# Sliding-window attention on one Trainium2 core: four tokens to an operation in place of two, and logits with a head's eight keys side by side

## The chip, the core and the metric

The kernel runs on one core of a Trainium2 chip. A core has five engines that run their own queues in order: TensorE (PE in the profile; PEld are its weight loads), VectorE (DVE), ScalarE (ACT), GpSimd (POOL) and SyncE (SP), which here issues all DMA transfers. They meet through semaphores. The metric is the device time of the whole program in microseconds. The kernel before took 1144.45 us (median of 3 runs, 1144.21 to 1144.93).

## What is computed

Two layers, each an attention A and an MLP B with residuals, over 2048 tokens of 640 features, in float32. Both layers use the same weights.

```python
def _A_ref(x, wqkv, wo):
    H = 32; Dh = D // H                      # 32 heads of 20
    W, dil = 8, 2
    ...
    idx = pos[:, None] - off[None, :]        # each token sees itself and 7 tokens before it, 2 apart
    ...
    logits = jnp.einsum("bhsd,bhswd->bhsw", q, kg) * scale
    logits = jnp.where(mask[None, None, :, :], logits, -1e9)
    attn = _softmax(logits, axis=-1)
    o = jnp.einsum("bhsw,bhswd->bhsd", attn, vg)
    return (lambda x, *d: x.transpose(*d))(o, 0, 2, 1, 3).reshape(B, S, D) @ wo

def _B_ref(x, w1, b1, w2, b2):
    y = _layernorm(x, axis=-1)
    h = _gelu(jnp.einsum("bsd,df->bsf", y, w1) + b1)
    return jnp.einsum("bsf,fd->bsd", h, w2) + b2

x = x + _A_ref(_layernorm(x, axis=-1), A_wqkv, A_wo)
x = x + _B_ref(_layernorm(x, axis=-1), B_w1, B_b1, B_w2, B_b2)
...
```

## The kernel before

The 2048 tokens of a layer are cut into four units of 512: the even and the odd tokens, in two halves each, since a window steps over every second token. A partition holds four neighbouring tokens of a unit (M = 4). Over the two layers there are eight units, n = 0 to 7. PE works in float16, and each float32 operand is split into a high and a low half: a product is three passes (high by high, high by low, low by high).

For each unit the kernel makes a layer norm, turns it by DMA transposes into `yT`, and multiplies by the query, key and value weights (L648). The result goes to a DRAM buffer (`spill`) and comes back with the seven tokens of halo (`fetch`, L690) in four groups of eight heads, 160 features each (GC = 160); the groups are numbered G = 4n + g, 0 to 31. There is one buffer for queries and keys (`qk`) and one for values (`v`).

Attention of a group runs on DVE. A pass over two tokens (EH = 2), eight keys and 160 features multiplies queries and keys (L732, 2560 elements per partition), and a reduce over the 20 features of a head gives the logits (L736). This is done for both pairs of tokens, in one of two product buffers `pr` each. Then come the mask (L741, in the units that hold the start of the sequence), the maximum over the keys (L744), the subtraction (L745), the exponential on ACT (L747), the sum (L749), its reciprocal (L750) and the product with it (L751). Logits lie token by token, key by key, head by head (`p t w h`), so these two reduces read a head's eight keys at a step of eight elements. The value product (L758) and three halving additions (L766 twice, L770) follow, again for each pair of tokens. ACT and GpSimd (or DVE for the last group, L780) split the result into halves, DMA transposes turn it, and PE multiplies by the output weights (L805, the projection).

The MLP walks over 12 blocks of 128 inner features: an inner product (L871), the GELU on ACT (L877), the high half on ACT (L880), the low half on DVE (L882), and the outer product (L892), whose passes with the high half of the inner block come first and the pass with the low half after. The first unit's MLP is done in two parts of two token tiles each (256 columns), and so has 24 splits L882 of 256 elements; the later ones take 512. The weights are split once at the start, on ACT and DVE (L475, L476), from staging buffers, and parked in DRAM. The last two units are multiplied together by another scheme (`pair`), which reuses the product buffers.

The order on each engine is made when the program is built: `Plan` takes each operation with an estimated duration, a priority and the keys that it needs and gives, and places at every step the operation that can start first, by priority among those ready. A DVE operation is estimated at 0.067 us and 960 elements a microsecond; `more=0.19` is added for the two strided reduces. GpSimd operations marked as a pair wait for a DVE operation with a single input. So a change of sizes moves the work on all engines.

Of the kernel before, what the change touches and what calls it, by code (L numbers as in the profile page):

```python
# [16 lines left out]
P = 128  # L17
# [17 lines left out]
LEAD = (3, 3)  # L35

EH = 2

# [252 lines left out]
def sliding_dilated_then_mlp_kernel(  # L291
# [25 lines left out]
    def many(pool, n, shape, dt, name):  # L317
        return [pool.tile(shape, dt, name=f"{name}{i}") for i in range(n)]
# [69 lines left out]
    for i, q in enumerate(("A12", "S1", "A22", "HL")):  # L388
# [3 lines left out]
        "wq": [("qkvp", last_n, t, g) for t in range(M) for g in range(NG)],  # L392
        "pr": [("o", 2 * NU * NG - 1, a) for a in range(M // EH)] + [("done", 0, i) for i in range(M)],
        "wo": [("wop", last_n, t, c) for t in range(M) for c in range(2)],
# [22 lines left out]
    def dve(n, prio, emit, need=(), give=(), use=(), more=0.0, wait=None):  # L417
        plan.add("dve", v_cost(n) + more, prio, emit, need, give, use, wait=wait, pair=give[0][0] in PAIRS)
# [123 lines left out]
    def layernorm(n, prio, yk, twice):  # L542
# [56 lines left out]
        for t in range(m):  # L599
# [23 lines left out]
            if twice and n != PAIR[0]:  # L623
                G, a = NG * n + ((6, 1), (7, 1), (8, 0), (8, 1))[t][0], (1, 1, 0, 1)[t]
                pool(ASIDE, -200 + n, lambda t=t: nc.gpsimd.tensor_add(x[u][:, t], x[u][:, t], b2),  # L625
                     need=[("y", name, t), ("qk", G, a), "b2"], give=[("xb", n, t)], pair=True)

# [72 lines left out]
    def attention(G):  # L700
        n, g = divmod(G, NG)
        la, u = divmod(n, NU)
        par, start, m = UNITS[u]
        E = EH * W * GC
        L = m * W * GH
        NE = m // EH
# [6 lines left out]
        def windows(w, t0, *dims):  # L713
            c = w[:, t0:t0 + EH]
            return bass.AP(tensor=c.tensor, offset=c.offset, ap=[list(c.ap[0]), [GC, EH], *dims])

        def lg(t0=0, t1=m):
            return tile_of(*sk)[:, t0 * W * GH:t1 * W * GH].rearrange("p (t w h) -> p t w h", t=t1 - t0, w=W)

        def lgt():  # L720
            return lg().rearrange("p t w h -> p t h w")
# [4 lines left out]
        for a in range(NE):  # L726
            t0 = a * EH
            pk = ("pr", (G, a, 0))

            def qk(t0=t0, pk=pk):  # L730
                w = tile_of(*wk)
                nc.vector.tensor_mul(tile_of(*pk), w[:, HALO + m + t0:HALO + m + t0 + EH, None, :].to_broadcast([P, EH, W, GC]),  # L732
                                     windows(w, t0, [GC, W], [1, GC]))

            dve(E, G - 0.6, qk, need=[("inq", G), ("ink", G)], give=[("qk", G, a)], use=[wk, pk, sk])
            dve(E, G - 0.7, lambda pk=pk, t0=t0: nc.vector.tensor_reduce(  # L736
                lg(t0, t0 + EH).rearrange("p t w h -> p (t w h)"), tile_of(*pk).rearrange("p t w (h d) -> p (t w h) d", d=DH),
                axis=AX.X, op=OP.add), need=[("qk", G, a)], give=[("lg", G, a)], use=[pk, sk])
        last = [("lg", G, a) for a in range(NE)]
        if start == 0:  # L740
            dve(L, G - 0.8, lambda: nc.vector.tensor_add(  # L741
                lg(), lg(), mask[:, :, :, None].to_broadcast([P, m, W, GH])), need=[*last, "mask"], give=[("lm", G)], use=[sk])
            last = [("lm", G)]
        dve(L, G - 0.8, lambda: nc.vector.tensor_reduce(mx(0), lgt(), axis=AX.X, op=OP.max), need=last, give=[("mx", G)], use=[sk], more=0.19)  # L744
        dve(L, G - 0.8, lambda: nc.vector.tensor_sub(lg(), lg(), mx(0)[:, :, None, :].to_broadcast([P, m, W, GH])),  # L745
            need=[("mx", G)], give=[("sub", G)], use=[sk])
        act(L, -450 + G, lambda: nc.scalar.activation(tile_of(*sk)[:, :L], tile_of(*sk)[:, :L], AF.Exp, scale=scale),  # L747
            need=[("sub", G)], give=[("e", G)], use=[sk], table="exp")
        dve(L, G - 0.8, lambda: nc.vector.tensor_reduce(mx(1), lgt(), axis=AX.X, op=OP.add), need=[("e", G)], give=[("s", G)], use=[sk], more=0.19)  # L749
        dve(8 * m * GH // 2, G - 0.8, lambda: nc.vector.reciprocal(mx(1), mx(1)), need=[("s", G)], give=[("rc", G)], use=[sk])  # L750
        dve(L, G - 0.8, lambda: nc.vector.tensor_mul(lg(), lg(), mx(1)[:, :, None, :].to_broadcast([P, m, W, GH])),  # L751
            need=[("rc", G)], give=[("at", G)], use=[sk])
        for a in range(NE):
            t0 = a * EH
            vk = ("pr", (G, a, 1))

            def pv(t0=t0, vk=vk):
                nc.vector.tensor_mul(  # L758
                    tile_of(*vk).rearrange("p t w (h d) -> p t (w h) d", d=DH),
                    lg(t0, t0 + EH).rearrange("p t w h -> p t (w h)")[:, :, :, None].to_broadcast([P, EH, W * GH, DH]),  # L760
                    windows(tile_of(*vw), t0, [DH, W * GH], [1, DH]))

            dve(E, G - 0.85, pv, need=[("at", G), ("inv", G)], give=[("pv", G, a)], use=[vw, sk, vk])
            last = ("pv", G, a)
            for w in (4, 2):
                dve(EH * w * GC, G - 0.9, lambda vk=vk, w=w: nc.vector.tensor_add(  # L766
                    tile_of(*vk)[:, :, 0:w], tile_of(*vk)[:, :, 0:w], tile_of(*vk)[:, :, w:2 * w]),
                    need=[last], give=[("ad", G, a, w)], use=[vk])
                last = ("ad", G, a, w)
            dve(EH * GC, G - 0.9, lambda vk=vk, t0=t0: nc.vector.tensor_add(  # L770
                ot()[:, t0:t0 + EH], tile_of(*vk)[:, :, 0], tile_of(*vk)[:, :, 1]),
                need=[last], give=[("o", G, a)], use=[vk, ok])

        def hi():
            return tile_of(*hk)[:, :, 0, g * GC:(g + 1) * GC]

        act(m * GC, -350 + G, lambda: nc.scalar.activation(hi(), ot(), AF.Copy),
            need=[("o", G, a) for a in range(NE)], give=[("oh", G)], use=[ok, hk])
        def lo(eng):
            eng.tensor_sub(tile_of(*hk)[:, :, 1, g * GC:(g + 1) * GC], ot(), hi())  # L780

        if g < NG - 1:
            pool(ASIDE, -300 + G, lambda: lo(nc.gpsimd), need=[("oh", G), ("qk", G + 1, 0)], give=[("ol", G)], use=[ok, hk],
                 pair=True)
        else:
            dve(m * GC, -300 + G, lambda: lo(nc.vector), need=[("oh", G)], give=[("ol", G)], use=[ok, hk])
# [561 lines left out]
```

## Time and profile before

| | |
|---|---|
| median of 3 runs | 1144.45 us |
| span of the profiled execution | 1146.1 us |
| granted TensorE clock, mean | 0.998 |
| DVE products L732 and L758 | 64 each, 2808 and 2818 ns |
| DVE reduce L736 | 64, 2801 ns |
| DVE additions L766 | 128, 1150 ns |
| moved by DMA | 235.47 MB, mean 205 GB/s |

The profiled execution is one run under the hardware profiler; its span is that of the program's instructions. A group of instructions has its line, engine, output and inputs by the program's names, the count, and the mean duration. Idle time of an engine matters only where another one waits for it.

### The profile page before, as it was taken

Reading aid. Unit: us, or ns where it says so; the run is one execution under the profiler, and the core shown is the slowest. Engines: PE = TensorE matmul, PEld = TensorE weight load, DVE = VectorE, ACT = ScalarE, POOL = GpSimd, SP = SyncE. Lnnn points to the kernel's source line nnn. Section 1 sums busy time; section 2 is a strip of 40 time slices with the busy share of each in tenths; the row PEclk is TensorE's granted clock in tenths of the full one; section 3 lists DMA queues with packets and bytes.
Section 4 is the critical chain, followed back from the end, with each engine's and each line's share of the span. In section 5 each row is a group of like instructions: output and inputs, shape, how many; then the busy total and the mean of one; then the engine's idle time right before and its main releaser. Section 6 shows DMA issues by size and latency. Waiting matters only on the chain.

```text
span 1146.1 us, 17470 instructions
## 1 busy us (share of the span) xinstructions
PE 1137.1 (99%) x6812; PEld 628.4 (55%) x6812; DVE 1038.4 (91%) x1028; ACT 606.6 (53%) x1131; POOL 113.2 (10%) x94
## 2 busy tenths in 40 slices
PE   9999999999999999999999999999999999999998
PEld 6444446567565465546555555556455556555476
DVE  7999999999899999999999999999999993847972
ACT  6485336536365275734537662479347445657720
POOL 1010000211111102110112012012111000000000
PEclk9999999999999999999999999999999999999999
DMA  9999998978976477576655965569686555974201
GB/s 318 307 299 266 329 302 244 321 264 244 239 189 232 140 221 213 178 207 198 186 187 176 221 190 164 175 188 192 164 247 183 175 171 156 217 239 122 65 24 69
DMA packets 239791, 235.47 MB, mean 205 GB/s; under 512 B 139020, under 2 KB 195164, under 8 KB 239708
## 3 DMA queue, kind: packets, MB, share of 16 engines
q1 hardware_dynamic: 239708, 234.36, 69.9%
q8 instruction: 53, 0.87, 0.3%
q14 instruction: 30, 0.25, 0.1%
HBM read 157.55 MB, written 44.78 MB: 177 GB/s over the span
## 4 chain that ended last, share of the span: by engine, by line
PE 72%; DVE 3%; DMA 1%; issue 0%; ACT 0%; DVEq 0%
PE acc L892 18%; PE ps L871 17%; PE ps L648 17%; PE ps L805 10%; PE acc L1073 4%; PE ps L1108 3%; PE ps L1073 2%; DMA yT<-w 1%; DVE yT L1020 1%; DVE pr L1005 1%; PE acc L1108 1%; DVE wq L1194 0%; DVE wq L1182 0%; DVE v L1195 0%; DVE xf L1196 0%
## 5 line engine op out<-in xcount | busy, mean ns | idle before, releaser
L648 PE MATMUL ps<-wq,yT 128*128 128x480 f16 (+1 forms) x1950 | 391.0, 363 | 1.5 <-DMA yT<-w 1.1
L648 PEld LDWEIGHTS <-yT 128*128 128x128 f16 x1950 | 189.3, 98 | 200.8 <-DMA yT<-w 1.4
L892 PE MATMUL acc<-c,act 128*128 128x512 f16 (+1 forms) x1728 | 249.3, 299 | 2.3 <-DMA c<-mw 1.6
L871 PE MATMUL ps<-yT,c 128*128 128x512 f16 (+1 forms) x1260 | 247.8, 350 | 0.0
L892 PEld LDWEIGHTS <-act 128*128 128x128 f16 x1728 | 136.1, 98 | 108.8 <-issue 1.9
L871 PEld LDWEIGHTS <-c 128*128 128x128 f16 x1260 | 120.9, 98 | 107.3 <-DMA c<-mw 0.3
L732 DVE TENSOR_TENSOR pr<-qk 128x2560 f32<-128x2560 f32 x64 | 179.5, 2808 | 0.0
L758 DVE TENSOR_TENSOR pr<-sm,v 128x2560 f32<-128x2560 f32 x64 | 179.1, 2818 | 0.3
L736 DVE TENSOR_REDUCE sm<-pr 128x128 f32<-128x2560 f32 x64 | 179.2, 2801 | 0.0
L665 ACT ACTIVATE ev<-ps 128x480 f32<-128x480 f32 x128 | 72.6, 568 | 177.2 <-PE ps L648 157.5
L877 ACT ACTIVATE act<-ps,b 128x512 f32<-128x512 f32 (+1 forms) x84 | 52.4, 624 | 172.9 <-PE ps L871 170.2
L766 DVE TENSOR_TENSOR pr<-pr 128x640 f32<-128x640 f32 (+1 forms) x128 | 143.1, 1150 | 0.3
L805 PE MATMUL ps<-wo,yT 128*128 128x320 f16 x960 | 131.7, 299 | 0.0
L805 PEld LDWEIGHTS <-yT 128*128 128x128 f16 x960 | 93.8, 98 | 37.4
L780 POOL TENSOR_TENSOR ohl<-w,ohl 128x640 f16<-128x640 f32 x24 | 34.9, 1456 | 425.9 <-DVE pr L732 171.6
L882 DVE TENSOR_TENSOR act<-act 128x512 f16<-128x512 f32 (+1 forms) x84 | 51.0, 609 | 16.0 <-ACT act L880 15.9
L587 POOL TENSOR_TENSOR ln<-ln,half 128x2 f32<-128x2 f32 (+1 forms) x31 | 36.2, 1173 | 276.6 <-ACT ln L584 276.6
L625 POOL TENSOR_TENSOR xf<-xf,b 128x640 f32<-128x640 f32 x24 | 37.3, 1558 | 144.6 <-DVE pr L732 58.4
L880 ACT ACTIVATE act<-act 128x512 f16<-128x512 f32 (+1 forms) x84 | 47.5, 565 | 3.4 <-PE acc L892 1.5
L610 ACT ACTIVATE w<-xf,ln 128x640 f32<-128x640 f32 x53 | 47.5, 909 | 2.7 <-DVE w L618 2.1
L570 ACT ACTIVATE junk<-xf 128x640 f16<-128x640 f32 x57 | 41.8, 733 | 12.9 <-DVE xf L814 8.0
L618 DVE TENSOR_TENSOR w<-w,w 128x640 f16<-128x640 f32 x56 | 45.7, 830 | 2.1 <-ACT w L616 2.1
(200 smaller groups left out, 984.1 us busy)
## 6 DMA issues: line engine op xcount, KB each, us to landing
c<-mw SPq DMA_DIRECT2D x174, 320.0 KB, 3.6
spill<-ev SPq DMA_DIRECT2D x64, 480.0 KB, 3.6
qk<-spill SPq DMA_DIRECT2D x32, 880.0 KB, 6.0
v<-spill SPq DMA_DIRECT2D x32, 880.0 KB, 5.3
qk<-spill SPq DMA_DIRECT2D x32, 320.0 KB, 3.6
act<-in_B_w_dram SPq DMA_DIRECT2D x24, 320.0 KB, 4.9
mw<-c SPq DMA_DIRECT2D x24, 320.0 KB, 4.7
pr<-in_B_w_dram SPq DMA_DIRECT2D x24, 320.0 KB, 4.1
```

The costliest lines, as they stand in the source:

```text
L648: nc.tensor.matmul(ps, transposed(yk)[:, a * KD + k, t * P:(t + 1) * P], wq[:, b, k, g, i0:i1], start=first and j == 0, stop=last and j == ...
L665: act(3 * GC, -400 + n, lambda i=i, pk=pk, ek=ek: nc.scalar.activation(tile_of(*ek)[:, :, i], tile_of(*pk)[:, :3 * GC].rearrange("p (a c) ...
L732: nc.vector.tensor_mul(tile_of(*pk), w[:, HALO + m + t0:HALO + m + t0 + EH, None, :].to_broadcast([P, EH, W, GC]), windows(w, t0, [GC, W], ...
L736: dve(E, G - 0.7, lambda pk=pk, t0=t0: nc.vector.tensor_reduce(lg(t0, t0 + EH).rearrange("p t w h -> p (t w h)"), tile_of(*pk).rearrange(" ...
L758: nc.vector.tensor_mul(tile_of(*vk).rearrange("p t w (h d) -> p t (w h) d", d=DH), lg(t0, t0 + EH).rearrange("p t w h -> p t (w h)")[:, :, ...
L766: dve(EH * w * GC, G - 0.9, lambda vk=vk, w=w: nc.vector.tensor_add(tile_of(*vk)[:, :, 0:w], tile_of(*vk)[:, :, 0:w], tile_of(*vk)[:, :, w ...
L805: nc.tensor.matmul(tile_of(*pk)[:, :D // 2], transposed(yk)[:, a * KD + k, t * P:(t + 1) * P], wo[:, b, k, c * D // 2:(c + 1) * D // 2], s ...
L871: nc.tensor.matmul(tile_of(*pk)[:, :nt], tile_of(*ck)[:, a, k * P:(k + 1) * P], transposed(yk)[:, c * KD + k, t0 * P:t1 * P], start=i == 0 ...
L877: act(nt, -430, lambda pk=pk, h32=h32, e=e: nc.scalar.activation(tile_of(*h32)[:, :nt], tile_of(*pk)[:, :nt], AF.Gelu_apprx_tanh, bias=b1[ ...
L882: dve(nt, -1000, lambda h32=h32, hk=hk: nc.vector.tensor_sub(tile_of(*hk)[:, 1, :nt], tile_of(*h32)[:, :nt], tile_of(*hk)[:, 0, :nt]), nee ...
L892: nc.tensor.matmul(accs[k][:, c0:c0 + n], tile_of(*hk)[:, a, (i - t0) * P:(i - t0 + 1) * P], tile_of(*wk)[:, c, w0:w0 + n], start=first, s ...
L1073: nc.tensor.matmul(tile_of(*to(i))[:, :HALF], hl()[:, a, i * P:(i + 1) * P], row(c), start=start and (a, c) == PASS[0], stop=(a, c) == PAS ...
```

## The change

Attention no longer works on pairs of tokens. One product buffer holds all four tokens, key by key (`pr`, 8 keys x 4 tokens x 160 features); its two halves by keys still serve as the two staging buffers elsewhere. The query-key product, the reduce, the value product and each of the additions are one operation over 5120, 5120, 5120, 2560, 1280 and 640 elements. The logits are laid out token by token, head by head, key by key (`p t h w`), so that a head's eight keys are neighbours; the first reduce writes them at a step of eight elements and the value product reads them so. The maximum and the sum read neighbouring elements and lose `more=0.19`. Keys in the plan lose their pair number, and with them the needs of GpSimd's operations.

```diff
-        "pr": many(sb, SLOTS["pr"], [P, EH, W, GC], FT, "pr"),
...
+    pr = sb.tile([P, W, M, GC], FT, name="pr")
+    T["pr"] = [pr[:, i * W // 2:(i + 1) * W // 2] for i in range(2)]
...
-                G, a = NG * n + ((6, 1), (7, 1), (8, 0), (8, 1))[t][0], (1, 1, 0, 1)[t]
+                G = NG * n + (6, 7, 8, 8)[t]
...
-        E = EH * W * GC
+        E = m * W * GC
...
+        def lg():
+            return tile_of(*sk)[:, :L].rearrange("p (t h w) -> p t h w", t=m, w=W)
+
+        def by_key():
+            return tile_of(*sk)[:, :L].rearrange("p (x w) -> p w x", w=W)
...
+        def heads():
+            return pr.rearrange("p w t (h d) -> p w (t h) d", d=DH)
...
+            nc.vector.tensor_mul(pr.rearrange("p w t c -> p w (t c)"),
+                                 w[:, HALO + m:HALO + 2 * m].rearrange("p t c -> p (t c)")[:, None, :].to_broadcast([P, W, m * GC]),
+                                 windows(w, [1, m * GC]))
...
+        dve(E, G - 0.7, lambda: nc.vector.tensor_reduce(by_key(), heads(), axis=AX.X, op=OP.add),
...
-        dve(L, G - 0.8, lambda: nc.vector.tensor_reduce(mx(0), lgt(), axis=AX.X, op=OP.max), need=last, give=[("mx", G)], use=[sk], more=0.19)
+        dve(L, G - 0.8, lambda: nc.vector.tensor_reduce(mx(0), lg(), axis=AX.X, op=OP.max), need=last, give=[("mx", G)], use=[sk])
...
+        dve(E, G - 0.85, lambda: nc.vector.tensor_mul(
+            heads(), by_key()[:, :, :, None].to_broadcast([P, W, m * GH, DH]), windows(tile_of(*vw), [DH, m * GH], [1, DH])),
+            need=[("at", G), ("inv", G)], give=[("pv", G)], use=[vw, sk, *vk])
+        last = ("pv", G)
+        for w in (4, 2):
+            dve(m * w * GC, G - 0.9, lambda w=w: nc.vector.tensor_add(pr[:, 0:w], pr[:, 0:w], pr[:, w:2 * w]),
...
+        dve(m * GC, G - 0.9, lambda: nc.vector.tensor_add(ot(), pr[:, 0], pr[:, 1]), need=[last], give=[("o", G)], use=[*vk, ok])
```

The planner's order moves with it. The lines of the changed kernel are numbered anew: L730 is the query-key product, L735 its reduce, L742 and L747 the maximum and the sum, L743 the subtraction, L751 the value product, L756 and L759 the additions, L869 the MLP split that was L882. In the rows, `sm` holds logits and weights, `pr` products, `act` the MLP's inner block.

DVE's queue in the second group of heads, before, from the maximum to the next product (the exponential on ACT stands between L745 and L749; L618 splits a layer norm's result):

```order
L744 TENSOR_REDUCE sm_90<-sm_90 128x32
L745 TENSOR_TENSOR sm_90<-sm_90 128x256
L618 TENSOR_TENSOR w_88<-w_85,w_88 128x640
L749 TENSOR_REDUCE sm_90<-sm_90 128x32
L750 RECIPROCAL sm_90<-sm_90 128x32
L751 TENSOR_TENSOR sm_90<-sm_90 128x256
L732 TENSOR_TENSOR pr_76<-qk_67 128x2560
```

And now, from the maximum L742 to the sum L747:

```order
L742 TENSOR_REDUCE sm_88<-sm_88 128x32
L759 TENSOR_TENSOR w_85<-pr 128x640
L743 TENSOR_TENSOR sm_88<-sm_88 128x256
L730 TENSOR_TENSOR pr<-qk_67 128x5120
L617 TENSOR_TENSOR w_84<-w_83,w_84 128x640
L475 SCALAR_TENSOR_TENSOR wo<-act,wo 128x640
L747 TENSOR_REDUCE sm_88<-sm_88 128x32
```

Between the subtraction and the sum stood one split of 640 elements; now a whole query-key product of the next group, a split L617 and a weight split L475 stand there.

DVE's queue at the first splits of the MLP, before:

```order
L758 TENSOR_TENSOR pr_77<-sm_90,v_68 128x2560
L882 TENSOR_TENSOR act<-act 128x256 x2
L766 TENSOR_TENSOR pr_77<-pr_77 128x2x640
L882 TENSOR_TENSOR act<-act 128x256
L766 TENSOR_TENSOR pr_77<-pr_77 128x2x320
L758 TENSOR_TENSOR pr_76<-sm_90,v_68 128x2560
L770 TENSOR_TENSOR w_85<-pr_77 128x320
L766 TENSOR_TENSOR pr_76<-pr_76 128x2x640
L745 TENSOR_TENSOR sm_89<-sm_89 128x256
L766 TENSOR_TENSOR pr_76<-pr_76 128x2x320
L732 TENSOR_TENSOR pr_77<-qk_67 128x2560
L882 TENSOR_TENSOR act<-act 128x256
```

And now:

```order
L730 TENSOR_TENSOR pr<-qk_67 128x5120
L869 TENSOR_TENSOR act<-act 128x256
L747 TENSOR_REDUCE sm_87<-sm_87 128x32
L735 TENSOR_REDUCE sm_88<-pr 128x8x32
L869 TENSOR_TENSOR act<-act 128x256
L748 RECIPROCAL sm_87<-sm_87 128x32
L742 TENSOR_REDUCE sm_88<-sm_88 128x32
L749 TENSOR_TENSOR sm_87<-sm_87 128x256
L743 TENSOR_TENSOR sm_88<-sm_88 128x256
L869 TENSOR_TENSOR act<-act 128x256
L751 TENSOR_TENSOR pr<-sm_87,v_68 128x5120
```

The first three splits stood within four rows, with one addition between. Now each of the first two has an operation over 5120 elements ahead of it.

DVE's queue from the thirteenth and fourteenth split (the first row with L882) to the seventeenth (the last row); L936 and L923 add the MLP's result to the residual, L767 splits the attention's result of a unit's last group. Before:

```order
L736 TENSOR_REDUCE sm_89<-pr_77 128x128
L882 TENSOR_TENSOR act<-act 128x256 x2
L936 SCALAR_TENSOR_TENSOR xf<-acc_101,xf 128x2x128
L936 SCALAR_TENSOR_TENSOR xf<-acc_97,xf 128x512
L882 TENSOR_TENSOR act<-act 128x256
L936 SCALAR_TENSOR_TENSOR xf<-acc_98,xf 128x512
L751 TENSOR_TENSOR sm_90<-sm_90 128x256
L758 TENSOR_TENSOR pr_76<-sm_90,v_68 128x2560
L882 TENSOR_TENSOR act<-act 128x256
L766 TENSOR_TENSOR pr_76<-pr_76 128x2x640
L766 TENSOR_TENSOR pr_76<-pr_76 128x2x320
L882 TENSOR_TENSOR act<-act 128x256
```

And now, where the last row holds the seventeenth and the eighteenth:

```order
L735 TENSOR_REDUCE sm_87<-pr 128x8x32
L869 TENSOR_TENSOR act<-act 128x256 x2
L923 SCALAR_TENSOR_TENSOR xf<-acc_100,xf 128x2x128
L923 SCALAR_TENSOR_TENSOR xf<-acc_96,xf 128x512
L923 SCALAR_TENSOR_TENSOR xf<-acc_97,xf 128x512
L767 TENSOR_TENSOR ohl_75<-w_83,ohl_75 128x4x160
L739 TENSOR_TENSOR sm_87<-sm_87,mask 128x256
L730 TENSOR_TENSOR pr<-qk_67 128x5120
L869 TENSOR_TENSOR act<-act 128x256 x2
L742 TENSOR_REDUCE sm_87<-sm_87 128x32
L735 TENSOR_REDUCE sm_88<-pr 128x8x32
L869 TENSOR_TENSOR act<-act 128x256 x2
```

A value product with its two additions stood ahead of the seventeenth split; now a query-key product and a reduce of the tenth group stand there, and the split L767 of the second unit.

More of the change, by code (lines that the diff above doesn't have):

```diff
@@ L35 @@
 LEAD = (3, 3)
-EH = 2
 FAST = {0: (0, 1, 2), 1: (0, 1, 2, 3)}
@@ L711, in ot, with windows @@
             return tile_of(*ok).rearrange("p (t c) -> p t c", t=m)
[L713 to L721, printed above, removed]
+        def windows(w, *dims):
+            return bass.AP(tensor=w.tensor, offset=w.offset, ap=[list(w.ap[0]), [GC, W], *dims])
@@ L740, in attention @@
+        dve(E, G - 0.6, qk, need=[("inq", G), ("ink", G)], give=[("qk", G)], use=[wk, *pk, sk])
+        dve(E, G - 0.7, lambda: nc.vector.tensor_reduce(by_key(), heads(), axis=AX.X, op=OP.add),
+            need=[("qk", G)], give=[("lg", G)], use=[*pk, sk])
+        last = [("lg", G)]
         if start == 0:
             dve(L, G - 0.8, lambda: nc.vector.tensor_add(
-                lg(), lg(), mask[:, :, :, None].to_broadcast([P, m, W, GH])), need=[*last, "mask"], give=[("lm", G)], use=[sk])
+                lg(), lg(), mask[:, :, None, :].to_broadcast([P, m, GH, W])), need=[*last, "mask"], give=[("lm", G)], use=[sk])
@@ L748, in attention @@
             need=[("sub", G)], give=[("e", G)], use=[sk], table="exp")
[L749 removed]
+        dve(L, G - 0.8, lambda: nc.vector.tensor_reduce(mx(1), lg(), axis=AX.X, op=OP.add), need=[("e", G)], give=[("s", G)], use=[sk])
         dve(8 * m * GH // 2, G - 0.8, lambda: nc.vector.reciprocal(mx(1), mx(1)), need=[("s", G)], give=[("rc", G)], use=[sk])
[L751 removed]
+        dve(L, G - 0.8, lambda: nc.vector.tensor_mul(lg(), lg(), mx(1)[:, :, :, None].to_broadcast([P, m, GH, W])),
@@ L774, in hi @@
+        last = ("pv", G)
+        for w in (4, 2):
+            dve(m * w * GC, G - 0.9, lambda w=w: nc.vector.tensor_add(pr[:, 0:w], pr[:, 0:w], pr[:, w:2 * w]),
+                need=[last], give=[("ad", G, w)], use=vk)
+            last = ("ad", G, w)
+        dve(m * GC, G - 0.9, lambda: nc.vector.tensor_add(ot(), pr[:, 0], pr[:, 1]), need=[last], give=[("o", G)], use=[*vk, ok])
         def hi():
@@ L777, in attention @@
         act(m * GC, -350 + G, lambda: nc.scalar.activation(hi(), ot(), AF.Copy),
-            need=[("o", G, a) for a in range(NE)], give=[("oh", G)], use=[ok, hk])
+            need=[("o", G)], give=[("oh", G)], use=[ok, hk])
         def lo(eng):
```

42 lines of the change are left out of this document (7 added, 35 removed).

## The prediction

> **What bounds the kernel now.** The page comes first: which engine is full, and who ends the chain.
>
> ```profile
> span 1146.1 us, 17470 instructions
> PE 1137.1 (99%) x6812; PEld 628.4 (55%) x6812; DVE 1038.4 (91%) x1028; ACT 606.6 (53%) x1131; POOL 113.2 (10%) x94
> ...
> PE 72%; DVE 3%; DMA 1%; issue 0%; ACT 0%; DVEq 0%
> ```
>
> TensorE (PE) is busy for all but 9.0 us of the span, and the change leaves its matmuls alone. What can be won is time in which PE stands still; what can be lost is new time of that kind. So the next view is the waits of PE, and with it the windows in which its busy time is short of 50.
>
> ```profile
> PE acc L892 <- DMA c<-mw: 1.6, 2, 1.3
> PE acc L1269 <- POOL ident L447: 1.3, 1, 1.3
> PE ps L648 <- DMA yT<-w: 1.1, 1, 1.1
> PE acc L892 <- DVE act L882: 0.7, 1, 0.7
> ```
>
> ```profile
> 50.00:100.00 50.00, 50.00 (x249) 24.17 (x247) 47.97 (x44) 40.31 (x86) 5.04 (x5) 1.00 0.98 291
> 100.00:150.00 50.00, 50.00 (x249) 24.16 (x247) 46.94 (x41) 16.72 (x29) 2.80 (x2) 1.00 0.96 322
> 150.00:200.00 50.00, 50.00 (x288) 27.99 (x287) 48.04 (x38) 27.82 (x61) 1.72 (x2) 1.00 0.88 263
> 200.00:250.00 50.00, 48.01 (x314) 29.87 (x313) 50.00 (x44) 23.40 (x43) 10.08 (x7) 0.97 0.91 286
> 250.00:300.00 50.00, 48.58 (x371) 33.04 (x370) 45.94 (x51) 24.93 (x50) 6.50 (x4) 1.00 0.93 252
> ```
>
> In each row the second number is PE's busy time, the fourth VectorE's (DVE), and the third from the end the granted clock. PE loses 1.99 us in 200:250, 1.5 us more there to a clock of 0.97 (3% of 50), and 1.42 us in 250:300: **4.9 us** in all, at the start of the first MLP block and just before the second layer's first product. DVE is idle for 7.05 us in 50:200 and not at all in 200:250. So DVE sets the pace here beside PE, and the change is about DVE.
>
> **The price of one DVE operation.** The timeline, start and duration in us:
>
> ```profile
> 229.17 2.82 DVE L758 TENSOR_TENSOR pr<-sm,v 128x2560 f32<-128x2560 f32 x1
> 231.90 0.48 DVE L770 TENSOR_TENSOR w<-pr 128x320 f32<-128x320 f32 x1
> 232.30 1.49 DVE L766 TENSOR_TENSOR pr<-pr 128x1280 f32<-128x1280 f32 x1
> 233.71 0.42 DVE L745 TENSOR_TENSOR sm<-sm 128x256 f32<-128x256 f32 x1
> 234.04 0.82 DVE L766 TENSOR_TENSOR pr<-pr 128x640 f32<-128x640 f32 x1
> 234.78 2.82 DVE L732 TENSOR_TENSOR pr<-qk 128x2560 f32<-128x2560 f32 x1
> ...
> 238.25 0.42 DVE L882 TENSOR_TENSOR act<-act 128x256 f16<-128x256 f32 x1
> 238.59 0.61 DVE L749 TENSOR_REDUCE sm<-sm 128x32 f32<-128x256 f32 x1
> 239.11 2.81 DVE L736 TENSOR_REDUCE sm<-pr 128x128 f32<-128x2560 f32 x1
> ...
> 242.17 0.35 DVE L750 RECIPROCAL sm<-sm 128x32 f32<-128x32 f32 x1
> 242.43 2.77 DVE L732 TENSOR_TENSOR pr<-qk 128x2560 f32<-128x2560 f32 x1
> ```
>
> The next operation starts about 0.08 us before the last one's duration is over, so I price by the step from start to start: 2.73 for 2560 elements, 1.41 for 1280, 0.74 for 640, 0.40 for 320, 0.33 for 256, 0.52 for the strided reduce of 256, 0.26 for the reciprocal. From 1.41 and 0.74 the part that doesn't grow with the elements is 0.07. A 5120-element operation, which the trace doesn't have, is then 2 x 2.73 - 0.07 = 5.39, between 5.34 (no fixed part at all) and 5.46 (twice the half); the low end is the nearer, since 1280 against 640 shows the fixed part is paid once.
>
> Fewer instructions: six pairs of a group become one each, 192 of 1028. A group cost 6 x 2.73 + 2 x (1.41 + 0.74 + 0.40) + 1.96 = 23.44 us (1.96 is the softmax: 0.52, 0.33, 0.52, 0.26, 0.33). It will cost 3 x 5.39 + 2.75 + 1.41 + 0.73 + 1.58 = 22.64, where the two reduces of the softmax now read side by side and are taken at 0.33 like L745. That is 0.80 a group, 25.6 us over 32 groups. [...] None of this is on the path by itself: PE's 1137.1 us covers it.
>
> An operation that needs the one just ahead of it takes longer:
>
> ```profile
> 292.89 0.62 DVE L744 TENSOR_REDUCE sm<-sm 128x32 f32<-128x256 f32 x1
> 293.54 0.42 DVE L745 TENSOR_TENSOR sm<-sm 128x256 f32<-128x256 f32 x1
> ```
>
> The step is 0.65 in place of 0.52, so 0.125 each. Ahead of the first MLP split 29 operations stand so in the old order and 9 in the new: 2.5 us saved.
>
> **What moves.** PE waits for DVE through the splits L882 (the low half of the MLP's inner block). In the new order 5.39 us pieces stand between them, and more attention stands ahead of them. Ahead of the first split the old queue has groups 0 to 4 whole, 15.61 us of group 5 and 11.44 of group 6: 144.2 us. The new one has groups 0 to 5 whole, 11.44 of group 6 and 5.39 of group 7: 152.7. Ahead of the seventeenth: 7 groups, 17.76 of the eighth and 5.46 of the ninth, 187.3, against 8 groups, 11.44 and 10.78, and one L780 at 0.74: 204.1. So the new queue is 8.4 and then 16.8 us longer at the same work of PE, 5.9 and **14.3** after the 2.5.
>
> ```profile
> 225.11 1.80 PE L871 MATMUL ps<-yT,c 128*128 128x256 f16 x15
> 226.02 0.76 DVE L882 TENSOR_TENSOR act<-act 128x256 f16<-128x256 f32 x2
> 226.74 2.55 PE L892 MATMUL acc<-c,act 128*128 128x512 f16 x17
> ...
> 277.29 0.42 DVE L882 TENSOR_TENSOR act<-act 128x256 f16<-128x256 f32 x1
> ...
> 282.48 1.79 PE L892 MATMUL acc<-c,act 128*128 128x512 f16 x12
> ...
> 284.11 0.60 PE L871 MATMUL ps<-yT,c 128*128 128x256 f16 x4
> ```
>
> The seventeenth split ended at 277.71. Eight of the 12 matmuls at 282.48 use the high half (12 take 1.63 us, so 1.09), so PE needed it at 283.57: 5.86 us to spare. 14.3 - 5.86 = 8.4 us late, less what DVE gets back of its idle time. At the first split 0.86 us was to spare (226.44 against 226.74 plus four matmuls, 0.54), and the 15 matmuls at 225.11, 1.63 us, now stand behind it: 5.9 - 0.86 + 1.63 = 6.7 late, less the same.
>
> How much comes back:
>
> ```profile
> DVE c L476 <- ACT c L475: 3.5, 6, 1.1
> DVE sm L749 <- ACT sm L747: 2.3, 4, 0.8
> DVE w L618 <- ACT w L616: 0.3, 1, 0.3
> ```
>
> These are DVE's waits between 50 and 200 us. The exponential's wait (2.3) is covered in the new order by a 5.39 us product from the second group on, so 1.8 of it goes. The weight splits' wait (3.5) goes where they stand behind more attention, as 19 of 29 do by at least part of an operation. Bounds: 1.8 (exponentials alone) and 7.05 (all idle time of the windows). I take **5.5**, nearest to the 6.1 that the three rows add up to, because attention fills most of these gaps.
>
> Sum: 8.4 - 5.5 = 2.9 us later at the seventeenth split than the old PE was, with the old stalls already in that time. The 1.42 us at 290 go, since the wait there (L648 for yT) falls behind a PE that is 2.9 us later. From there DVE only gains on PE. Total +1.5 us on the profiled 1146.1, or 1147.6; that execution is 1.65 above the median of 1144.45, so **1146.0**: no change. What a measurement of this kernel can tell from no change is 0.2%, 2.3 us.
>
> At nothing I cost: GpSimd's adds (10% busy; the reduce that lets them in is now one of 5.39), the tail (attention ends earlier, the last products still run through PE), and the copies ACT makes. If that cover were gone, a GpSimd add of some 1.5 us would be late once a unit, eight times.
>
> **Rivals.** *Faster:* the splits are late nowhere, and all 4.9 us go: 1139.6. It takes DVE regaining more than the 8.4, beyond its 7.05 us of idle, or ACT being late as well; with half of the 4.9, 1142.0. For it speaks that the new PE order puts the first low-half matmuls ahead of a product that could have filled a wait. I give it 0.19.
>
> *Slower, at the MLP start:* the weights arrive no earlier (DMA share 0.96 to 0.98), so only the 1.8 comes back: 8.4 - 1.8 - 1.4 = +5.2, 1149.7. It is slower by over 0.2% from a return under 4.7 on. The third unit's projection is a second place of this kind:
>
> ```profile
> 405.01 0.82 DVE L780 TENSOR_TENSOR ohl<-w,ohl 128x640 f16<-128x640 f32 x1
> ...
> 413.27 6.79 PE ps L805 x50
> ```
>
> 7.4 us lie between DVE's last piece and PE; PE comes 22.3 us of matmuls sooner, DVE's queue is 14.9 shorter (12.4 by these prices and the 2.5), so nothing is left but the returned 5.5 and PE's own lateness, for the transposes that stand between. Chance 0.29.
>
> *The layout costs what it saves:* logits are now written, and weights read, at a step of eight elements, as L749 reads them: 0.52 against 0.33, 0.19 for 256 elements. Taken once for each reduce and each value product, 18 stand ahead of the seventeenth split: 3.4 us, 1149.4. Against it: each such element is followed by 19 more cycles of the same. Chance 0.10. [...] That the softmax reduces stay at 0.52 would be the same 3.0 us by the eighth group, and is counted in this chance.
>
> **How the numbers follow.** The forecast has 0.42. Same is 0.40 of it; faster 0.20, the faster rival and a sliver of the forecast; slower 0.40, the two slower rivals and another sliver. The range goes from a little beyond half of the faster rival, 1141.0, to 1152.5, which is the slower rival with the layout's 3.4 less a little.
>
> **What the new profile would show.** A 5120-element step of 5.39 and a group of 22.6 us, DVE at about 1012 busy (1038.4 - 25.6). PE short by some 5 to 7 us in 200:300 with DVE's L869 as releaser, and full afterwards. If PE stands nowhere in 200:300, the return was underrated; if it stands at projections near 390 to 520, the second place decides; if the value product's step is over 5.5, the layout does.

## The result and the profile after

The changed kernel took 1153.43 us (median of 4 runs, 1151.19 to 1153.65) against 1144.38 for the kernel before: a ratio of 1.0071, 95% interval 1.0059 to 1.0084. It is slower by 0.7%. The forecast was 1146.0 and the range ended at 1152.5. The profiled execution took 1151.19 us, with a span of 1149.4. Each run of the changed kernel has both numbers, and in all of them the time is the span and about 1.8 us.

The page of the changed kernel, the busy times and the products:

```profile
span 1149.4 us, 17270 instructions
...
PE 1136.1 (99%) x6812; PEld 627.4 (55%) x6812; DVE 1024.6 (89%) x836; ACT 603.7 (53%) x1129; POOL 152.0 (13%) x94
...
L730 DVE TENSOR_TENSOR pr<-qk 128x5120 f32<-128x5120 f32 x32 | 175.5, 5484 | 19.9 <-DMA qk<-spill 19.5
...
L751 DVE TENSOR_TENSOR pr<-sm,v 128x5120 f32<-128x5120 f32 x32 | 175.8, 5492 | 0.4
L735 DVE TENSOR_REDUCE sm<-pr 128x256 f32<-128x5120 f32 x32 | 175.3, 5477 | 0.2
...
L767 POOL TENSOR_TENSOR ohl<-w,ohl 128x640 f16<-128x640 f32 x24 | 59.2, 2465 | 400.1 <-DVE pr L730 223.1
...
L617 DVE TENSOR_TENSOR w<-w,w 128x640 f16<-128x640 f32 x56 | 50.9, 924 | 7.0 <-ACT w L615 6.9
```

DVE does less (1024.6 busy after 1038.4) with 192 instructions fewer, and PE's work is the same. The span has 13.3 us without PE, 4.3 more than before. PE's waits and windows in the changed kernel:

```profile
PE acc L879 <- DVE act L869: 6.0, 5, 3.0
...
PE acc L879 <- ACT act L867: 0.9, 1, 0.9
PE ps L858 <- DMA c<-mw: 0.6, 1, 0.6
```

```profile
50.00:100.00 50.00, 50.00 (x249) 24.15 (x248) 49.10 (x34) 39.29 (x84) 6.41 (x5) 1.00 1.02 303
100.00:150.00 50.00, 50.00 (x249) 24.15 (x248) 49.79 (x33) 18.64 (x33) 3.25 (x2) 1.00 1.00 297
150.00:200.00 50.00, 50.00 (x288) 28.05 (x287) 49.46 (x32) 29.42 (x66) 2.00 (x2) 1.00 0.92 276
200.00:250.00 50.00, 45.57 (x302) 27.54 (x300) 49.86 (x37) 24.71 (x43) 8.26 (x7) 1.00 0.99 312
250.00:300.00 50.00, 46.86 (x380) 34.05 (x379) 48.83 (x43) 22.47 (x48) 12.09 (x4) 1.00 0.88 252
```

PE is short by 4.43 and 3.14 us in the last two rows, 7.57 in all, at the start of the first MLP block, and the split L869 releases it in five of the waits. DVE's idle time between 50 and 200 went from 7.05 to 1.65, so 5.4 us came back. The timeline of DVE shows what each late split stands behind:

```profile
222.57 5.49 DVE L730 TENSOR_TENSOR pr<-qk 128x5120 f32<-128x5120 f32 x1
227.98 0.42 DVE L869 TENSOR_TENSOR act<-act 128x256 f16<-128x256 f32 x1
228.31 0.41 DVE L747 TENSOR_REDUCE sm<-sm 128x32 f32<-128x256 f32 x1
228.64 5.48 DVE L735 TENSOR_REDUCE sm<-pr 128x256 f32<-128x5120 f32 x1
234.04 0.41 DVE L869 TENSOR_TENSOR act<-act 128x256 f16<-128x256 f32 x1
...
248.47 5.49 DVE L751 TENSOR_TENSOR pr<-sm,v 128x5120 f32<-128x5120 f32 x1
253.88 1.95 DVE L869 TENSOR_TENSOR act<-act 128x256 f16<-128x256 f32 x2
...
287.94 0.75 DVE L869 TENSOR_TENSOR act<-act 128x256 f16<-128x256 f32 x2
```

The last row holds the seventeenth split. And PE's timeline, with its idle time in brackets:

```profile
225.72 1.26 PE L879 MATMUL acc<-c,act 128*128 128x512 f16 x8 [0.93 <-ACT act L867]
228.46 1.80 PE L879 MATMUL acc<-c,act 128*128 128x512 f16 x12 [1.47 <-DVE act L869]
...
234.51 2.53 PE L879 MATMUL acc<-c,act 128*128 128x512 f16 x16 [0.97 <-DVE act L869]
...
255.56 0.72 PE L879 MATMUL acc<-c,act 128*128 128x512 f16 x4 [2.98 <-DVE act L869]
...
287.49 1.79 PE L879 MATMUL acc<-c,act 128*128 128x512 f16 x12
```

The first wait is for the high half, which ACT makes (L867). Each of the three waits for L869 ends with a split that had a 5.4 us operation ahead of it. The longest has something more: two splits take 1.95 us where two others take 0.75. GpSimd's timeline has the reason:

```profile
248.61 6.61 POOL L767 TENSOR_TENSOR ohl<-w,ohl 128x640 f16<-128x640 f32 x1 [17.45 <-DVE sm L749]
```

Such a subtraction takes 1.40 us at its shortest and 1.64 in the median of the 24. This one came 0.14 us after the value product and ended 1.3 us after it, so it seems to have been held by the product, and the split by it. One profile cannot tell that from a late start; an experiment can.

### The profile page after: what moved, and what is told of

It reads as the page before. It is cut to its first block, busy times and chain, and to the rows that moved or that the text cites. A ratio compares the mean times of both kernels' runs of the same rounds, so it can differ in the third digit from the quotient of the medians.

```text
span 1149.4 us, 17270 instructions
## 1 busy us (share of the span) xinstructions
PE 1136.1 (99%) x6812; PEld 627.4 (55%) x6812; DVE 1024.6 (89%) x836; ACT 603.7 (53%) x1129; POOL 152.0 (13%) x94
## 4 chain that ended last, share of the span: by engine, by line
PE 89%; DVE 7%; issue 2%; ACT 1%; DMA 0%; SPq 0%; DVEq 0%; ACTq 0%
PE ps L647 31%; PE acc L879 19%; PE ps L858 19%; PE ps L792 11%; PE acc L1060 3%; PE ps L1095 3%; PE ps L1060 2%; DVE pr L992 1%; DVE pr L756 1%; DVE pr L751 1%; DVE pr L730 1%; DVE sm L735 1%; DVE yT L1007 1%; PE acc L1095 1%; DMA xf<-in_A_x_dram 0%
## 5 line engine op out<-in xcount | busy, mean ns | idle before, releaser
L730 DVE TENSOR_TENSOR pr<-qk 128x5120 f32<-128x5120 f32 x32 | 175.5, 5484 | 19.9 <-DMA qk<-spill 19.5
L751 DVE TENSOR_TENSOR pr<-sm,v 128x5120 f32<-128x5120 f32 x32 | 175.8, 5492 | 0.4
L735 DVE TENSOR_REDUCE sm<-pr 128x256 f32<-128x5120 f32 x32 | 175.3, 5477 | 0.2
L756 DVE TENSOR_TENSOR pr<-pr 128x2560 f32<-128x2560 f32 x64 | 140.8, 2200 | 0.2
L767 POOL TENSOR_TENSOR ohl<-w,ohl 128x640 f16<-128x640 f32 x24 | 59.2, 2465 | 400.1 <-DVE pr L730 223.1
L586 POOL TENSOR_TENSOR ln<-ln,half 128x2 f32<-128x2 f32 (+1 forms) x31 | 50.0, 1616 | 320.5 <-ACT ln L583 320.5
L869 DVE TENSOR_TENSOR act<-act 128x512 f16<-128x512 f32 (+1 forms) x84 | 53.0, 640 | 13.5 <-ACT act L867 13.1
L617 DVE TENSOR_TENSOR w<-w,w 128x640 f16<-128x640 f32 x56 | 50.9, 924 | 7.0 <-ACT w L615 6.9
L624 POOL TENSOR_TENSOR xf<-xf,b 128x640 f32<-128x640 f32 x24 | 38.2, 1601 | 85.3 <-DVE pr L730 39.3
L867 ACT ACTIVATE act<-act 128x512 f16<-128x512 f32 (+1 forms) x84 | 47.4, 565 | 1.8
```

The source lines that it names most:

```text
L730: nc.vector.tensor_mul(pr.rearrange("p w t c -> p w (t c)"), w[:, HALO + m:HALO + 2 * m].rearrange("p t c -> p (t c)")[:, None, :].to_broa ...
L735: dve(E, G - 0.7, lambda: nc.vector.tensor_reduce(by_key(), heads(), axis=AX.X, op=OP.add), need=[("qk", G)], give=[("lg", G)], use=[*pk, sk])
L751: dve(E, G - 0.85, lambda: nc.vector.tensor_mul(heads(), by_key()[:, :, :, None].to_broadcast([P, W, m * GH, DH]), windows(tile_of(*vw), [ ...
L756: dve(m * w * GC, G - 0.9, lambda w=w: nc.vector.tensor_add(pr[:, 0:w], pr[:, 0:w], pr[:, w:2 * w]), need=[last], give=[("ad", G, w)], use=vk)
L869: dve(nt, -1000, lambda h32=h32, hk=hk: nc.vector.tensor_sub(tile_of(*hk)[:, 1, :nt], tile_of(*h32)[:, :nt], tile_of(*hk)[:, 0, :nt]), nee ...
```

## Experiments

Three theories were open. **Layout:** the new writes and reads cost time. **Long pieces:** operations of 5.4 us hold up the splits, in any order. **Order:** the planner, given other durations, comes out with an order that is worse around the first MLP block. Beside these stood the GpSimd subtraction, and the question how far the two profiled executions stand for their kernels. The kernel before was timed again beside each of three sets of runs, with medians of 1144.87, 1144.73 and 1144.91 us; the last run below stands beside a single one of 1143.74.

### Both kernels again

> The kernel before, unchanged, for a second profile. All four executions of the changed kernel took 1.75 to 1.8 us more than their span. If that holds for the old kernel too, the profiled execution with its span of 1146.1 took about 1147.9, and was 3.4 us above its median, and the 3.41 us in which PE was short in 200:300 and the dip of the clock were of that execution alone. Theory 'typical execution has no stalls': this profile has a span of 1142.4 to 1143.2 and PE is short by under 1.0 us in 200:300. Theory of the prediction, that these stalls are the kernel's own: span 1145.5 to 1146.5, PE short by about 3.4 us there again. Time 1144.4 by both.

> The changed kernel, unchanged, for a second profile: its first one has a span of 1149.4 where three other executions had 1151.6 to 1151.9. [...] Time 1153.4.

The kernel before: 1145.15 us (10 runs, 1144.02 to 1148.53). Its profiled execution was the slowest of the ten, 1148.53. Its span, and its windows:

```profile
span 1146.8 us, 17470 instructions
```

```profile
200.00:250.00 50.00, 48.83 (x337) 30.94 (x335) 50.00 (x44) 24.31 (x45) 10.14 (x7) 1.00 0.94 298
250.00:300.00 50.00, 47.17 (x355) 31.67 (x354) 46.81 (x51) 24.34 (x49) 6.43 (x4) 1.00 0.90 245
```

PE is short by 4.0 us there, and by 1.52 in 400:450. Read alone, this is the profile of the other theory, that the stalls are the kernel's own. But the other nine executions have spans of 1142.2 to 1144.9. This one has 10.8 us of span without PE, 5.5 of them in these stalls; if nothing else differs, a span of 1142.2 has room for only 0.9 us of stalls, and one of 1144.9 for 3.6. So the stalls differ from execution to execution, and both profiles of the old kernel are of executions that have many of them. This is worked out from the spans: no quick execution of this kernel was profiled.

The changed kernel: 1151.95 us (4 runs, 1151.25 to 1154.24), ratio 1.0066 (1.0051 to 1.0081). PE is short by 7.6 us in 200:300, at the same places, and by 0.3 in 500:550. This execution (1151.64) is one of the quick ones too, so where the longer ones lose 2.2 to 2.6 us more than the profiled execution of their set was not seen.

### Layout and order, each alone

The layout alone, with two tokens to an operation:

```diff
-        "pr": many(sb, SLOTS["pr"], [P, EH, W, GC], FT, "pr"),
+        "pr": many(sb, SLOTS["pr"], [P, W, EH, GC], FT, "pr"),
...
-            return tile_of(*sk)[:, t0 * W * GH:t1 * W * GH].rearrange("p (t w h) -> p t w h", t=t1 - t0, w=W)
+            return tile_of(*sk)[:, :L].rearrange("p (t h w) -> p t h w", t=m, w=W)
...
-        dve(L, G - 0.8, lambda: nc.vector.tensor_reduce(mx(0), lgt(), axis=AX.X, op=OP.max), need=last, give=[("mx", G)], use=[sk], more=0.19)
+        dve(L, G - 0.8, lambda: nc.vector.tensor_reduce(mx(0), lg(), axis=AX.X, op=OP.max), need=last, give=[("mx", G)], use=[sk])
```

> The layout alone: products key by key and logits with a head's eight keys side by side, but two tokens to an operation as before. Theory 'pieces' (the loss comes from operations of 5.4 us between the splits and from their order): 1143.5 to 1145, no change or a little faster, DVE busy about 12 us less than before (64 strided reduces at 0.19). Theory 'layout' (the strided writes and reads cost, or the order that the cheaper reduces bring): 1149 to 1153.

1150.04 us, ratio 1.0044 (1.0028 to 1.0059): taken by itself a win for "layout". But PE's waits name another releaser:

```profile
PE ps L874 <- DMA c<-mw: 4.3, 2, 3.0
```

Weights for the first block land late; the row names no DVE operation. The planner had lost its 0.19 for the two reduces (the last pair of lines of the diff), and with it the order had changed. So the layout and the order were taken apart. The kernel before without the 0.19 has in every queue, row by row, the order of the layout run (the sum's line L749 is changed in the same way):

```diff
-        dve(L, G - 0.8, lambda: nc.vector.tensor_reduce(mx(0), lgt(), axis=AX.X, op=OP.max), need=last, give=[("mx", G)], use=[sk], more=0.19)
+        dve(L, G - 0.8, lambda: nc.vector.tensor_reduce(mx(0), lgt(), axis=AX.X, op=OP.max), need=last, give=[("mx", G)], use=[sk])
```

The layout run with the 0.19 kept has the order of the kernel before:

```diff
-        dve(L, G - 0.8, lambda: nc.vector.tensor_reduce(mx(0), lg(), axis=AX.X, op=OP.max), need=last, give=[("mx", G)], use=[sk])
+        dve(L, G - 0.8, lambda: nc.vector.tensor_reduce(mx(0), lg(), axis=AX.X, op=OP.max), need=last, give=[("mx", G)], use=[sk], more=0.19)
```

> The kernel before with its own instructions and layout; only the planner's extra 0.19 for the two strided reduces is dropped, and with that every queue has exactly the order of the run with the layout alone (1150.0). Theory 'order' (the change's loss is that the planner, given other durations, comes out with another order around the first MLP block): 1149 to 1152, PE short by 4 to 7 us in 225:275. Theory 'layout' (the new writes and reads cost): 1144 to 1146 as before.

> The layout alone again, with the planner's extra 0.19 kept for the two reduces, which no longer need it: every queue has exactly the order of the kernel before, and DVE does the same work in some 12 us less (64 reduces at 0.19). Theory 'order': 1143 to 1145, PE short by no more than before in 225:300. Theory 'layout': 1149 to 1152.

| | order of the kernel before | order without the 0.19 |
|---|---|---|
| laid out by token and key | 1144.73 | 1156.56, ratio 1.0107 (1.0091 to 1.0122) |
| laid out by head | 1144.32, ratio 0.9996 (0.9987 to 1.0006) | 1150.04, ratio 1.0044 (1.0028 to 1.0059) |

Down each column the new layout is no slower, and in the right one faster by 6.5 us; along the rows the new order costs 11.8 and 5.7. "Layout" falls. The run at 1156.56 went past the 1152 that was expected. A likely reason, which no run tests, is that DVE there needs the time that its order was planned without. Its waits:

```profile
PE ps L805 <- ACT ps L817: 4.4, 2, 3.9
PE ps L871 <- DMA c<-mw: 3.7, 2, 2.3
```

The second is the place of the layout run, the first one, after 700 us, is its own. The layout run in the old order is the nearest to a profile of a quick execution of the old kernel, with less work on DVE:

```profile
span 1142.4 us, 17470 instructions
...
PE 1136.0 (99%) x6812; PEld 628.2 (55%) x6812; DVE 1027.6 (90%) x1028; ACT 606.9 (53%) x1131; POOL 114.1 (10%) x94
```

```profile
200.00:250.00 50.00, 49.45 (x341) 31.32 (x340) 49.59 (x44) 24.36 (x46) 9.97 (x7) 1.00 0.95 302
250.00:300.00 50.00, 49.74 (x369) 32.99 (x368) 49.03 (x53) 25.06 (x50) 6.44 (x4) 1.00 0.92 261
```

DVE gained 10.8 us on the kernel before and nothing came of it: PE is short by 0.81 us in 200:300, and there is no more to win.

### The merge alone, and the merge from group 12 on

Four tokens to an operation in the old layout (the 0.19 kept):

```diff
-    pr = sb.tile([P, W, M, GC], FT, name="pr")
+    pr = sb.tile([P, M, W, GC], FT, name="pr")
```

> The merge alone: four tokens to an operation, logits and products laid out token by token, key by key, as before. Theory 'pieces': 1152 to 1156, as the changed kernel or some us more, since DVE keeps the two strided reduces (0.19 each, 7 groups ahead of the middle of the first block: 2.7 us), and PE short by 7 to 11 us in 200:300. Theory 'layout': 1143.5 to 1146.

1154.22 us, ratio 1.0081 (1.0066 to 1.0096), the time that "pieces" gave. PE is short by 6.3 us in 200:300, less than the 7 that was its least, at a granted clock of 0.90 in 200:250, and the longest wait is for weights once more.

```profile
PE acc L877 <- DMA c<-mw: 4.9, 1, 4.9
...
PE acc L877 <- DVE act L867: 1.3, 1, 1.3
```

SyncE's own waits between 205 and 240 tie a part of this to a long operation:

```profile
SPq L689 <- DVE pr L748: 1.5, 1, 1.5
```

A load of values (L689) stood on SyncE's queue for 1.5 us, until the value product L748 had ended, and was issued at 222.48. The weights that PE waited for were issued behind it, at 223.33, and PE's wait ended at 231.28. So "pieces" has at most 1.5 of those 4.9 us; the rest was not taken apart.

Then the changed kernel with groups 0 to 11 in pairs:

```diff
+HALVED = range(12)
...
+        NE = 2 if G in HALVED else 1
+        EH = m // NE
```

> The changed kernel's layout everywhere, but groups 0 to 11 two tokens to an operation (with the planner's 0.19, so that the queues up to the first MLP block are as before), and groups 12 to 31 four tokens. Theory 'the first MLP block alone': the operations of 5.4 us cost nothing later, where PE has a spare operation at hand: 1143.5 to 1146. Rival 'long pieces delay PE everywhere': 1148 to 1153, with PE short after 450.

> The run with two tokens to an operation in groups 0 to 11 and four from group 12 on, with the same order on every queue; only the half of the product buffer that a pair takes is now the one that the planner gave it. 1145 to 1147, PE short by under 1 us in 200:300 and by about 2 us in 350:500, as in the run with the other halves.

In the first of the two a pair takes a half of the product buffer that the other pair may still use, so the attention of groups 0 to 11 isn't the reference's; the second mends that. 1146.01 (ratio 1.0012, 1.0003 to 1.0021) and 1146.38 us (1.0014, 1.0005 to 1.0023). With the old order and pairs up to the first block about four fifths of the loss are gone. That places the loss, but does not part the order from the long operations, since both are gone there. In the second, PE is short by 1.42 us in 200:300, more than the 1 us expected, and by 1.97 in 350:500, where the groups of four have begun (the product of group 12 is at 381):

```profile
PE acc L893 <- DVE xf L937: 1.5, 1, 1.5
```

### The GpSimd subtraction

The subtraction of group 6 waits for a later product; all queues keep their order:

```diff
-            pool(ASIDE, -300 + G, lambda: lo(nc.gpsimd), need=[("oh", G), ("qk", G + 1)], give=[("ol", G)], use=[ok, hk],
+            pool(ASIDE, -300 + G, lambda: lo(nc.gpsimd), need=[("oh", G), ("qk", G + 1 + (G == 6))], give=[("ol", G)], use=[ok, hk],
```

> The changed kernel with the same order on every queue; one GpSimd operation, the subtraction L767 of group 6, waits for the query product of group 8 and so runs beside a reduce, in place of beside the value product L751 at 248. Theory 'port' (the subtraction held L869 up by 1.2 us at 255): L767 there about 1.4 us and not 6.61, the two splits at 254 take 0.75 and not 1.95 us, the 3.05 stall of PE is 1.2 us shorter, 1150 to 1151. Rival 'the 5.4 us product alone sets that stall': the stall stays at about 3, time 1151.5 to 1153.5.

The name "port" is the author's guess at a cause, which no run shows; the runs show how long the operations took. 1150.57 us (1149.85 to 1151.04), ratio 1.0048 (1.0035 to 1.0061). GpSimd, DVE and PE, a fence each:

```profile
267.04 1.45 POOL L767 TENSOR_TENSOR ohl<-w,ohl 128x640 f16<-128x640 f32 x1 [35.04 <-DVE act L869]
```

```profile
249.33 5.49 DVE L751 TENSOR_TENSOR pr<-sm,v 128x5120 f32<-128x5120 f32 x1
254.74 0.75 DVE L869 TENSOR_TENSOR act<-act 128x256 f16<-128x256 f32 x2
```

```profile
226.63 1.25 PE L879 MATMUL acc<-c,act 128*128 128x512 f16 x8 [0.99 <-DMA c<-mw]
229.31 3.18 PE L879 MATMUL acc<-c,act 128*128 128x512 f16 x12 [1.43 <-DVE act L869]
...
241.75 1.79 PE L879 MATMUL acc<-c,act 128*128 128x512 f16 x12 [0.25 <-DMA c<-mw]
...
255.21 0.72 PE L879 MATMUL acc<-c,act 128*128 128x512 f16 x4 [1.87 <-DVE act L869]
```

The subtraction takes 1.45, the splits 0.75, and PE's wait is 1.87 where it was 2.98 and 3.05: 1.1 to 1.2 us of it were the subtraction's. That is shown by the rows. The change of the time points the same way, but its interval overlaps that of the changed kernel.

### The same instructions in another order

The changed kernel, with the planner's patience and DMA look-ahead set otherwise:

```diff
-HURRY = {3: 0.9, 7: 0.9, 11: 0.9}
+HURRY = {3: 3.0, 4: 1.5, 7: 0.0, 11: 0.5}
...
-    AHEAD = 3.0
+    AHEAD = 3.8
```

> The changed kernel's instructions, every one of them and on the same engines, in another order: the planner's patience ahead of the operations of groups 3, 4, 7 and 11 is 3.0, 1.5, 0 and 0.5 us (0.9, 0.6, 0.9 and 0.9 before), and its DMA look-ahead 3.8 in place of 3.0. On DVE the last weight split and the last layer norm halves of the first MLP unit no longer stand behind the value product of group 5, and the first two splits L869 no longer behind the query product of group 7. Theory 'order': the merge itself costs nothing, 1143.5 to 1147, PE short by under 4 us in 200:300. Rival 'long pieces': operations of 5.4 us hold the splits up in any order, 1149.5 to 1153.

> The changed kernel's instructions with one number of the planner changed, its DMA look-ahead 4.8 in place of 3.0, which puts groups 5 and 6 otherwise around the first MLP block. Theory 'order': a time of its own, away from the 1152 of the changed kernel by over 2 us, here 1146 to 1150. Rival 'long pieces': 1151 to 1154 as the changed kernel.

> The run with the other order again, for a second profile: its first profiled execution was the fastest of eleven (1145.55, median 1147.34). Theory 'DMA' (what is left of the loss is weights that land later in some executions): 1146 to 1149.5, and what PE is short of beyond the first profile's 2.7 us in 200:300 has DMA as releaser. Rival 'pieces' (splits L869 behind products of 5.4 us, a bit later or earlier): the excess has L869 as releaser.

The other order took 1147.34 us (11 runs, 1145.55 to 1149.35), ratio 1.0021 (1.0012 to 1.0030). Its windows, and what is left of the waits for the split:

```profile
200.00:250.00 50.00, 48.88 (x336) 30.86 (x335) 49.77 (x38) 18.19 (x36) 6.21 (x4) 1.00 0.89 292
250.00:300.00 50.00, 48.44 (x392) 34.69 (x390) 49.78 (x42) 24.46 (x50) 5.56 (x4) 1.00 0.92 258
```

```profile
PE acc L879 <- DVE act L869: 0.9, 2, 0.5
```

PE is short by 2.68 us after 7.57, with every operation of 5.4 us still there. So 4.6 us of the time (1151.95 less 1147.34) are order alone, with what it moves on GpSimd; 2.4 us above the kernel before are left, where "order" had the merge cost nothing. With the look-ahead at 4.8 and nothing else changed it took 1151.39, ratio 1.0056 (1.0042 to 1.0069): the time that "long pieces" gave and not the one that "order" gave, though its waits are others:

```profile
PE acc L879 <- DMA c<-mw: 2.6, 2, 2.3
PE ps L792 <- ACT ps L804: 2.0, 1, 2.0
```

The second profile of the other order took 1147.26, and PE is short by 2.0 us in 200:300, 0.4 in 300:350 and 0.7 in 500:700, of which a transpose by DMA is 0.7 and the split 0.5. Neither theory on the rest is borne out: it is spread thin. Whether four tokens can be had at the time of the kernel before in some order is open.

## Why the prediction was wrong

**What bounds the kernel: half right.** PE is the bound, and DVE beside it up to the first block. The 4.9 us of stalls were read from the profile correctly, but a typical execution of the kernel before has fewer. In its second profile they come to 5.5 us at a span of 1146.8; the median of the runs beside it has a span of 1143.1, which leaves room for 1.8. The nearest profile, the layout run in the old order, has 0.8. So 0.8 to 1.8 is an estimate.

**The prices: right, the busy time not.** A 5120-element operation steps by 5.41 (222.57 to 227.98); 5.39 was worked out. DVE was to be busy for 1012.8 us and was for 1024.6. The missing 11.8 lie partly in splits that ran beside a GpSimd operation: L617 takes 924 ns on average after 830, 5.2 us over 56, and every row of L617 that overlaps an L767 or L624 of GpSimd is longer, as at 882.68 with 2.02 us where the median is 0.815. The rest was not taken apart.

**What moves: right in kind, too small in size.** Attention ahead of the splits grew, 5.4 us of idle time came back (5.5 was taken), and L869 became PE's main releaser in 200:300. The seventeenth split started 10.65 us later than before (277.29, now 287.94), where 14.3 - 5.5 = 8.8 was worked out. The matmuls with its high half started at 287.49 after 282.48, with 1673 matmuls recorded ahead of them in both profiles: PE was 5.0 us later, and not 2.9. It did not wait at that split, which had about 0.2 us to spare by then; it had lost the time at earlier ones, most of it between 224 and 256. The stalls at 290 went, as forecast, and the second place that was named, the projections near 400, had no wait in the first profile and one of 0.3 us in the second.

**GpSimd's adds at nothing: wrong.** The prediction priced the loss of that cover at "some 1.5 us". One subtraction, of 6.61 us beside a value product and 1.45 beside a reduce, cost PE 1.1 to 1.2 us, over half of the 2.1 between 2.9 and 5.0. It was not the only one held: three more L767, each begun beside a value product, took 6.16 to 6.61 us, without a wait of PE behind them; in the kernel before none took over 1.69. ACT's copies, put at nothing too, come with one wait of 0.9.

**The step that failed is the last of the sum: "Total +1.5 us on the profiled 1146.1, or 1147.6; that execution is 1.65 above the median".** The 1.65 compares a span with a time. The execution took 1.8 us more than its span, as the runs with both numbers do, so it was about 1147.9, and 3.4 to 3.5 above its median. That slip alone changes nothing, since 1147.9 would also stand in place of 1146.1. What fails is carrying the 1.5 over to the median: it counts only what comes on top of 4.9 us of old stalls, and the median execution has most likely no more than 0.8 to 1.8 of them. The loss by medians falls into three pieces:

| us | first runs | both kernels again |
|---|---|---|
| from profiled execution to profiled execution | 3.3 | 3.1 |
| profiled execution above its median, kernel before | 3.5 | 3.7 |
| profiled execution below its median, changed kernel | 2.2 | 0.3 |
| loss by medians | 9.0 | 7.1 |

The 3.3 and the 3.5 take 1147.9 for the old kernel's profiled execution. The first piece is the sum's 1.5 and 1.8 more, of which the subtraction is 1.1 to 1.2. The second is the step that failed, and the largest in both columns. The third is the longer executions of the changed kernel, whose cause is open. With the first piece mended the forecast would have been 1147.8, with the second too about 1151.3, beside the 1153.43 and 1151.95 measured.

**The rivals.** "Slower at the MLP start" came, by another way than it was argued: the return of idle time was as forecast, not the small 1.8. "The layout costs what it saves" is refuted: the reduce L735 that writes at a step of eight and the product L751 that reads so take 5477 and 5492 ns beside 5484 for L730, and in the old order the layout alone is level with the kernel before. "Faster" had 0.8 to 1.8 us to win in a typical execution, and not 4.9.

**What the prediction didn't see** is that the queue lengths which it compared are one outcome of the planner among many. It took the new order as what the merge brings. The same instructions in two orders are 4.6 us apart, and the kernel before loses 11.8 by an order alone. What the merge costs apart from the order is about the 2.4 us left in that other order (1147.34 less 1144.91), or less, if a better order exists.

## What to carry to other kernels

Before stalls of one profiled execution are used as the base of a sum, hold its time (span and what lies around it) against the spread of the runs: where it is above the median by as much as its stalls, they are the execution's and not the kernel's. Where a planner lays out the queues from estimated durations, a change of a duration is also a change of order, and the order has to be tested by itself: the same order with the new instructions, and the old instructions in the new order. Where an operation of DVE holds a GpSimd operation, as the value product does here (6.61 us in place of 1.45 beside a reduce), the GpSimd operation should be let in beside one that doesn't.

## What the runs showed of the hardware

**Behind a product that held a GpSimd operation, DVE's next operation took longer too.** The subtraction at 248.61 took 6.61 us beside L751, and ended at 255.22, 1.26 us after the product. The two splits behind L751 stood next on DVE's queue and started at 253.88; together they took 1.95 us in place of 0.75. Beside a reduce the same subtraction took 1.45, and the splits 0.75. It shows once more at 365.36: L767 takes 6.61 us beside L751, 1.25 beyond the product's end, and the split of 512 elements behind that product takes 1.89, where the mean of such splits is 0.71. What makes the split longer is not shown.

**PE's granted clock fell after some stalls and not after others as long.** In the run with the later subtraction, waits of 0.99 and 1.43 us within 4 us are followed by 12 matmuls in 3.18 us, where 12 take 1.79; the granted clock is 0.93 in 225:250. In the changed kernel waits of 0.93 and 1.47 us, at the same two places, are followed by 12 in 1.80, at a clock of 1.00 in 225:250. After 2.98 us without work its four matmuls at 255.56 take 0.72, at a clock of 1.00 in 250:275. In the first profile of the kernel before, waits of 0.73 and 1.26 us are followed by 15 matmuls in 3.16 us at 240.81, with a clock of 0.54 in 240:242. The layout run shows a stall of 3.03 with slower matmuls behind it, at a clock of 0.93 in 225:250, 15 in 2.85 against 1.81:

```profile
227.87 1.81 PE L874 MATMUL ps<-yT,c 128*128 128x256 f16 x15 [1.31 <-DMA c<-mw]
...
234.34 2.85 PE L874 MATMUL ps<-yT,c 128*128 128x256 f16 x15 [3.03 <-DMA c<-mw]
```

The length of the waits doesn't part these cases: 2.42 us in two waits came with a lower clock in one run, and 2.40 in another did not; one wait of 3.03 us did, and one of 2.98 did not. What decides is not shown. Where the clock fell, the matmuls right behind the stall took 1.0 to 1.4 us longer (2.85 against 1.81, 3.18 against 1.79, 3.16 against 1.80), so a stall at the start of the block cost PE that much beyond its own length there.
